# Sink scores as column tiles inside the score task, a re-planned opening, and a four-slot load ring in a fused attention and MLP kernel

## The chip, the cores and the metric

The kernel runs on one core of one Trainium2 chip. The metric is the device time of one execution in microseconds (us). A ratio between two kernels is the mean time of one kernel's fast runs over the mean of the other's in the same rounds, so it is not quite the ratio of the medians quoted beside it; its 95% interval stands in brackets. "Faster" and "slower" need 2%, which is 4.8 us here.

A word on noise: the kernel before, run again with every batch, spread from 240.66 to 242.19 us, and its median of a batch from 241.2 to 241.56.

## The reference

Four batches of eight heads, 768 positions of 64 dimensions. Each query sees a causal window of 128 keys and the first four keys of its sequence, the sinks. The attention's output goes through a layer norm and an MLP (512 to 2048, relu, back to 512), and is added to the MLP's result.

```python
scores = scale * np.matmul(q, k.transpose(0, 1, 3, 2))
is_sink = pos[None, :] < int(n_sink)                  # n_sink = 4
in_window = (rel >= 0) & (rel < int(window))          # window = 128
scores = np.where(is_sink | in_window, scores, -1e9)
a = softmax(scores); x = np.matmul(a, v)              # [B, S, H*D]
# ... then
xn = (x - mu) / np.sqrt(var + 1e-06) * g_ln
out = x + np.maximum(xn @ w_ch1, 0.0) @ w_ch2
```

## The kernel before

The work is cut into 24 blocks of 128 positions (six per batch), in six groups of four. A block loads query, key and value (float32 to bfloat16, one queue that GpSimd feeds), transposes query and key on TensorE into a bank of PSUM (the memory that this kernel's matmuls write to), copies them out, forms the scores of its own and the previous block's keys, takes exponentials on ScalarE, multiplies with the values, normalises on VectorE, subtracts the mean, and transposes the result for the MLP. The MLP of a group is 32 quanta of four 512-column matmuls each. The attention of the next groups is interleaved with those quanta. Blocks 0 to 3 have no MLP to hide behind; I call their stretch the opening.

What makes this kernel special is that the order is not written by hand. A small planner runs while the program is built. It knows an estimated cost of each task, a lag between engines, the slots of each ring of buffers and an estimated landing time of each load, and it always takes the task that can start first:

```python
for e, c in t["engines"].items():
    start = max([at, free[e]] + [done[d][1] if done[d][0] == e else done[d][2] for d in t["deps"]])
    k = (round(start, 3), t["prio"], start + c, i, e)
    if best is None or k < best:
        best = k
# ...
if t["land"] is not None:                     # a load
    dma_free = max(dma_free, start + 1.5) + t["land"]
    end = dma_free + 0.5
```

The result is a fixed list of instructions for each engine. Each engine runs its list in that order.

The parts that the change touches, cut:

```python
RINGS = dict(pa=4, ps=2, ld=10, qk=5, ks=2, vs=2, e=8, es=3, ...)   # pa: PSUM banks, ld: loads, qk: transposed tiles

def pk_(e, s, s2):                            # sink scores: a task of their own, full array
    for hp in range(4):
        nc.tensor.matmul(P["pk", t], lhsT=ks_of[b][:, hp], rhs=qkT[t][:, 0, hp, :],
                         start=(hp == 0), stop=(hp == 3))
# ... loads: blocks 0 to 3, W1 in four quarters, W2 in four quarters, then
for t in range(4, NT):
    load_block(t)
# ... pacing: the transposes of block t wait for an MLP quantum
for t in range(4, NT):
    n = 8 * (t - 4) - 8
    if n >= 0:
        plan.tasks[d_t[t]]["deps"].append(quanta[n])
```

The softmax here doesn't subtract the row's maximum and nothing guards it: scores larger than these inputs give would overflow.

## Time and profile before

| | before |
|---|---|
| time, median of 3 runs | 241.26 us (241.13 to 241.31) |
| span of the profiled run | 239.8 us |
| TensorE busy, and its share of the chain that ended last | 96%, 93% |
| first MLP matmul starts | 27.09 us |
| last matmul starts | 235.24 us |

TensorE is the bound as a whole, but a busy TensorE can be full of dummy matmuls (line L166, written to fill planned gaps), as in the opening. After 27.09 us nearly all of TensorE's time is work. The two ends of that stretch, the start of the first MLP matmul and of the last matmul, are the two numbers to follow: the opening is what lies before the first, and the stretch between them is 235.24 - 27.09 = 208.15 us. The tail after the last one is a VectorE operation and a store.

### The profile page before, as it was taken

Reading aid. Unit: us, or ns where it says so; the run is one execution under the profiler, and the core shown is the slowest. Engines: PE = TensorE matmul, PEld = TensorE weight load, DVE = VectorE, ACT = ScalarE, POOL = GpSimd, SP = SyncE. Lnnn points to the kernel's source line nnn. Section 1 sums busy time; section 2 is a strip of 40 time slices with the busy share of each in tenths; the row PEclk is TensorE's granted clock in tenths of the full one; section 3 lists DMA queues with packets and bytes.
Section 4 is the critical chain, followed back from the end, with each engine's and each line's share of the span. In section 5 each row is a group of like instructions: output and inputs, shape, how many; then the busy total and the mean of one; then the engine's idle time right before and its main releaser. Section 6 shows DMA issues by size and latency. Waiting matters only on the chain.

```text
span 239.8 us, 4795 instructions
## 1 busy us (share of the span) xinstructions
PE 231.4 (96%) x1957; PEld 129.4 (54%) x1989; DVE 137.5 (57%) x393; ACT 118.8 (50%) x179; POOL 76.3 (32%) x93
## 2 busy tenths in 40 slices
PE   8899999999999999999999999999999999999993
PEld 5676644666555555555556555456555555444441
DVE  7485801599997848746647568656667547200121
ACT  2167366655486632186751385643385760166000
POOL 8994237998989542340000000001000000100000
PEclk9999999999999999999999999999999999999998
DMA  7999999999999975991002110002110001200112
GB/s 46 138 162 205 206 204 158 151 178 183 182 179 153 126 52 107 109 105 7 3 8 80 46 44 4 0 2 88 44 48 0 3 0 67 77 34 0 44 44 87
DMA packets 82583, 20.23 MB, mean 84 GB/s; under 512 B 75393, under 2 KB 79489, under 8 KB 82562
## 3 DMA queue, kind: packets, MB, share of 16 engines
q0 software_dynamic: 79104, 13.64, 72.9%
q1 hardware_dynamic: 3458, 6.30, 7.1%
q8 instruction: 15, 0.25, 0.4%
q14 instruction: 6, 0.05, 0.1%
HBM read 27.27 MB, written 6.29 MB: 140 GB/s over the span
## 4 chain that ended last, share of the span: by engine, by line
PE 93%; DVE 4%; issue 1%; POOL 1%; POOLq 0%
PE ph L568 35%; PE pc L594 35%; PE ps L379 5%; PE pt L323 5%; PE px L531 3%; PE po L472 2%; PE po L475 2%; PE pk L447 2%; PE po L468 2%; PE ps L370 1%; DVE xc L500 1%; PE pt L166 1%; PE pv L427 0%; POOL qkn L255 0%; DVE xt L488 0%
## 5 line engine op out<-in xcount | busy, mean ns | idle before, releaser
L568 PE MATMUL ph<-xnt,w1s 128*128 128x512 bf16 x369 | 88.1, 379 | 0.9 <-issue 0.2
L594 PE MATMUL pc<-w2s,h 128*128 128x512 bf16 x367 | 87.1, 379 | 1.0 <-issue 0.2
L581 ACT ACTIVATE h<-ph 128x512 bf16<-128x512 f32 x85 | 50.8, 597 | 51.9 <-PE ph L568 51.9
L568 PEld LDWEIGHTS <-w1s 128*128 128x128 bf16 x384 | 35.5, 98 | 38.8
L594 PEld LDWEIGHTS <-h 128*128 128x128 bf16 x384 | 35.4, 98 | 37.0
L397 ACT ACTIVATE e<-ps 128x1024 bf16<-128x1024 f32 (+1 forms) x48 | 43.8, 955 | 18.2 <-PE ps L379 17.8
L606 DVE SCALAR_TENSOR_TENSOR ot<-pc,rsg,xt 128x512 f32<-128x512 f32 x24 | 18.0, 748 | 44.3 <-PE pc L594 35.3
L520 POOL TENSOR_TENSOR rsg<-ve,eps_half 128x4 f32<-128x4 f32 x6 | 6.5, 1086 | 96.2 <-DVE ve L518 96.2
L255 POOL DMA_DIRECT2D qkn<-in_q_dram x24 | 22.0, 916 | 22.8 <-PE pt L323 16.0
L329 ACT COPY qkT<-pt 128x1024 bf16<-128x1024 bf16 (+1 forms) x19 | 15.9, 862 | 16.9 <-PE pt L323 16.8
L260 POOL DMA_DIRECT2D qkn<-in_k_dram x24 | 21.9, 914 | 5.2 <-DMA w2s<-in_moe_w_ch_dram 3.4
L263 POOL DMA_DIRECT2D vn<-in_v_dram x24 | 22.0, 919 | 3.5 <-DMA w1s<-in_moe_w_ch_dram 1.7
L488 DVE SCALAR_TENSOR_TENSOR xt<-po,rc 128x256 bf16<-128x256 f32 x48 | 20.4, 424 | 1.7
L500 DVE SCALAR_TENSOR_TENSOR xc<-xt,sums,gb 128x512 bf16<-128x512 bf16 x24 | 18.0, 751 | 0.8
L406 DVE TENSOR_TENSOR e<-e,mask_std 128x1024 bf16<-128x1024 bf16 x28 | 18.1, 682 | 0.0
L485 DVE RECIPROCAL rc<-po 128x4 f32<-128x4 f32 x48 | 8.6, 179 | 14.6 <-PE po L475 12.5
L323 PE MATMUL pt<-ident,qkn 128*128 128x128 bf16 x192 | 16.0, 226 | 0.9 <-DVE qkT L329 0.9
L472 PE MATMUL po<-vn,e 128*128 128x65 bf16 x192 | 16.9, 194 | 0.0
L472 PEld LDWEIGHTS <-e 128*128 128x128 bf16 x192 | 14.4, 99 | 3.8
L509 DVE BATCH_NORM_STATS2 st<-xt 128x6 f32<-128x512 bf16 x24 | 16.3, 680 | 0.0
L579 DVE TENSOR_SCALAR h<-ph 128x512 bf16<-128x512 f32 x11 | 7.6, 688 | 15.1 <-PE ph L568 15.0
L329 DVE COPY qkT<-pt 128x512 bf16<-128x512 bf16 (+1 forms) x13 | 6.4, 502 | 16.6 <-PE pt L323 16.6
(75 smaller groups left out, 190.4 us busy)
## 6 DMA issues: line engine op xcount, KB each, us to landing
out_dram<-ot SPq DMA_DIRECT2D x24, 256.0 KB, 2.0
qkn<-in_q_dram POOLq DMA_DIRECT2D x24, 128.0 KB, 6.1
qkn<-in_k_dram POOLq DMA_DIRECT2D x24, 128.0 KB, 6.2
vn<-in_v_dram POOLq DMA_DIRECT2D x24, 128.0 KB, 6.1
w1s<-in_moe_w_ch_dram POOLq DMA_DIRECT2D x4, 512.0 KB, 10.6
w2s<-in_moe_w_ch_dram POOLq DMA_DIRECT2D x4, 512.0 KB, 17.8
g_row<-in_moe_g_ln_dram SPq DMA_DIRECT2D x1, 2.0 KB
```

Source lines behind the costliest of these rows:

```text
L255: nc.gpsimd.dma_start(qn[t][:, 0], q[b, :, rows, :].rearrange("h p d -> p h d"))
L260: nc.gpsimd.dma_start(qn[t][:, 1], k[b, :, rows, :].rearrange("h p d -> p h d"))
L263: nc.gpsimd.dma_start(vn[:, t, :, 0:64], v[b, :, rows, :].rearrange("h p d -> p h d"))
L323: nc.tensor.transpose(P["pt", t][:, aa, hp, :], qn[t][:, aa, 2 * hp:2 * hp + 2, :], ident)
L329: (nc.scalar.copy if e == "ACT" else nc.vector.tensor_copy)(qkT[t][:, sl], P["pt", t][:, sl])
L397: nc.scalar.activation(E[t, half][:, :, :, 0:nkb, :], P["ps", t, half][:, :, :, 0:nkb, :], AF.Exp, scale=scale)
L472: nc.tensor.matmul(po[:, hh, :], lhsT=ee[:, h % 2, hh // 2, 0, :], rhs=vn[:, t, h, :], start=(r < 2 and hh == 0), stop=(r == 0), skip_grou ...
L488: nc.vector.scalar_tensor_tensor(xt[t][:, 256 * half:256 * half + 256].rearrange("p (h d) -> p h d", h=4), in0=po[:, :, 0:64], scalar=1.0, ...
L500: nc.vector.scalar_tensor_tensor(xc[t], in0=xt[t], scalar=sums[t][:, 2:3], in1=gb, op0=ALU.subtract, op1=ALU.mult)
L568: nc.tensor.matmul(ph, lhsT=w1s[:, j, 128 * ht:128 * (ht + 1)], rhs=xnt[g][:, j, 0:n], start=(j == 0), stop=(j == NDM - 1))
L581: nc.scalar.activation(o, i, AF.Relu)
L594: nc.tensor.matmul(P["pc", t], lhsT=h1[g, ht][:, 128 * ti:128 * (ti + 1)], rhs=w2s[:, ht, :], start=(ht == 0), stop=(ht == NH1 - 1))
```

## The change

The intent: take TensorE cycles out of the sink scores by giving the four-key products only a 32-column slice of the array each, so that four run side by side; keep them in the score task; shorten the opening; and free the transposes from the pacing, so that fewer load buffers are needed. I call the way in which the array is divided its mode: the full array, row tiles (the scores, which use 64 rows each), or column tiles (the new sink scores). The diff, cut to its core:

```diff
-    RINGS = dict(pa=4, ps=2, ld=10, qk=5, ...)
+    LDN, QKN = 4, 5
+    RINGS = dict(pa=4, ps=2, ld=LDN, qk=QKN, ...)
 ...  # planner: rings counted one by one, a limit on queued descriptors, landing constants
-                for n_, (ring, key, readers) in enumerate(t["take"]):
+                for ring, key, readers in t["take"]:
+                    n_ = seen[ring] = seen.get(ring, -1) + 1
-                end = dma_free + 0.5
+                end = dma_free + (0.6 if t["lag"] is None else t["lag"])
 ...  # opening: the gain's broadcast and most masks after the first query; more warm-up dummies
+        g_ = plan.add({"PE": 1.0}, [d_q[0]], g1, (0, 0, 3), take=[("pa", "gb", 1)])
+        D["mb"] = plan.add({"DVE": .45}, [d_q[0]], make_masks_b, (0, 0, 1))
+        D["mc"] = plan.add({"DVE": 1.3}, [d_q[0]], make_masks_c, (0, 1, 5))
 ...  # query and key of the split blocks get a PSUM bank each
-            tk = plan.add({"PE": .23}, [d_k[t], tq], tr(1), (0, t, 1), drop=[("ld", t)])
-            ck = plan.add({"DVE": .43, "ACT": .59}, [tk, cq], cp(1), (0, t, 0), drop=[("pt", t)])
+            tk = plan.add({"PE": .23}, [d_k[t], tq], tr(1), (0, t, 1), take=[("pa", ("pt", t, 1), 1)], drop=[("ld", t)])
+            ck = plan.add({"DVE": .43, "ACT": .59}, [tk], cp(1), (0, t, 0), drop=[("pt", t, 1)])
 ...  # sink scores: behind the scores, in the same task, eight column tiles
+                if len(slots) > len(halves):
+                    for h2 in range(2):
+                        for hp in range(4):
+                            nc.tensor.matmul(P["pk", t][32 * hp:32 * hp + 32, h2, :], lhsT=ks_of[b][:, h2, hp, :],
+                                             rhs=qkT[t][:, 0, hp, :], start=(h2 == 0), stop=True,
+                                             skip_group_check=True)
 ...  # sink values: two half-width matmuls in place of one
-                    nc.tensor.matmul(po, lhsT=ES[t], rhs=vs_t[b][:, 4 * half:4 * half + 4, :],
-                                     start=True, stop=False, skip_group_check=True)
+                    for h2 in range(2):
+                        nc.tensor.matmul(po.rearrange("p (j a) c -> p j a c", a=2)[:, :, h2, :], lhsT=ES[t][:, h2, :],
+                                         rhs=vs_t[b].rearrange("p (j a) c -> p j a c", a=2)[:, 2 * half:2 * half + 2, h2, :],
+                                         start=(h2 == 0), stop=False, skip_group_check=True)
 ...
-    WARM0 = 24
+    WARM0 = 34
+    SINK = .16
 ...  # pacing: the scores, not the transposes
-            plan.tasks[d_t[t]]["deps"].append(quanta[n])
+            plan.tasks[d_s[t]]["deps"].append(quanta[n])
```

## The prediction

> **What bounds the kernel now.** I read the page first (busy shares, the chain's shares), then the table of stretches, then TensorE's order of time in the opening and in one steady stretch, then the end of the chain.
>
> ```profile
> span 239.8 us, 4795 instructions
> ...
> PE 231.4 (96%) x1957; PEld 129.4 (54%) x1989; DVE 137.5 (57%) x393; ACT 118.8 (50%) x179; POOL 76.3 (32%) x93
> ...
> PE 93%; DVE 4%; issue 1%; POOL 1%; POOLq 0%
> ```
>
> TensorE is busy for 96% and is 93% of the chain; no other engine passes 57%. The stretches (length, busy time of each engine, granted clock, DMA) show where the rest is:
>
> ```profile
> 5.60:12.60 7.00, 6.09 (x53) 4.59 (x53) 3.66 (x19) 1.19 (x2) 7.00 (x9) 1.00 2.14 136
> 12.60:27.10 14.50, 14.07 (x224) 10.05 (x223) 10.26 (x37) 9.19 (x13) 8.39 (x11) 1.00 1.43 190
> 27.10:38.00 10.90, 10.85 (x50) 4.94 (x52) 3.07 (x9) 6.92 (x12) 3.50 (x4) 1.00 1.44 197
> 38.00:100.00 62.00, 61.37 (x592) 35.85 (x602) 47.10 (x133) 34.26 (x53) 47.21 (x53) 1.00 1.92 147
> 100.00:208.00 108.00, 106.91 (x896) 58.72 (x911) 65.81 (x172) 56.37 (x83) 5.73 (x6) 1.00 0.14 34
> ```
>
> From 27.1 on TensorE is full. I checked this against its own work: 16 MLP matmuls of 512 columns take 68.97 to 72.44 in the steady lines below, 217 ns each, so 768 take 166.5 us; blocks 4 to 23 add about 40 us (per full block: transposes 0.45, sink scores 0.22, scores 0.55, value matmuls 0.71, transposes of the normalised rows 0.22). Sum 206.3 us against 235.64 - 27.5 = 208.1 us. Under 2 us of idling is left there, so a change of order can't gain more than that after 27 us; only fewer TensorE cycles can. The opening is different:
>
> ```profile
> 7.50 0.58 PE L323 MATMUL pt<-ident,qkn 128*128 128x128 bf16 x4 [0.91 <-DVE qkT L329]
> 7.88 1.06 PE L166 MATMUL pt<-ident 128*128 128x128 bf16 x8
> ...
> 17.07 0.67 PE L166 MATMUL pk<-ident 128*128 128x128 bf16 x9
> ...
> 24.14 1.61 PE L166 MATMUL px<-ident 128*128 128x128 bf16 x26
> 26.08 0.40 PE L531 MATMUL px<-ident,xc 128*128 128x128 bf16 x4 [0.33 <-DVE xc L500]
> 26.32 0.78 PE L166 MATMUL ph<-ident 128*128 128x128 bf16 x11
> 27.09 3.18 PE L568 MATMUL ph<-xnt,w1s 128*128 128x512 bf16 x13
> ```
>
> L166 is dummy work that fills planned gaps: 36+15+9+11+9+3 = 83 of them in the groups by form, at least 83 x 56 ns = 4.6 us. So the busy digit of the opening is not work, and the first MLP matmul comes at 27.09. The end is fixed: last matmul ends at 235.64, then 0.75 us of VectorE and a store, 4.1 us, untouched by the change.
>
> **What the Trainium skill says.** "TensorE: Matmul & The Clock Gate", section on packing small matmuls: outputs on different 32-partition strips of PSUM run at the same time in the array; it gives 2.38x for three column tiles. Nothing in this trace has column tiles, but the row-tiled scores do overlap: 16 of them in 0.55 us is 34 ns each with the switches, half of the 56 ns a 128-column matmul costs. "TensorEngine Tiling (Array Packing)", Key Properties: changing the tiling mode drains TensorE; Restrictions: column tiling switches the fast weight load off. The trace agrees on the drain:
>
> ```profile
> 67.88 0.39 PE L531 MATMUL px<-ident,xc 128*128 128x128 bf16 x4
> 68.10 0.39 PE L447 MATMUL pk<-qkT,ks 128*128 128x128 bf16 x4
> 68.42 0.62 PE L379 MATMUL ps<-qkT 64*128 64x128 bf16 x16
> 68.97 3.63 PE L568 MATMUL ph<-xnt,w1s 128*128 128x512 bf16 x16
> ```
>
> Start to start, four transposes take 0.22, but four sink scores ahead of row-tiled scores take 0.32, so 0.10 is the switch in; eight pairs of scores would take 0.45 and take 0.55, so another 0.10 is the switch out. The clock gate of the same TensorE page (half rate until some 3.4 us of sustained work) also shows, though the clock column reads 1.00 throughout: 8 dummies at 7.88 have a spacing of (1.06 - 0.29)/7 = 110 ns, 9 at 17.07 one of (0.67 - 0.22)/8 = 56 ns. The opening is planned with warm costs but runs cold for its first third.
>
> **The change, part by part.**
>
> Sink scores. Removed per block with sinks (16 of 24): four 128-column matmuls in the full array, 4 x 56 = 224 ns, in a task of their own. Added: eight matmuls of 32 output columns behind the scores, which at four at a time are two rounds of 56 = 112 ns, plus one more switch of mode, estimated from the 0.10 above. That is 0.21 against 0.22: nothing, if the switch costs in full. If row tiles to column tiles drain less (TensorE has to leave the row-tiled mode anyway), up to 0.11 is gained. I take 0.05 per block: 16 x 0.05 = 0.8 us, 0.7 of it in the steady part. The two half-width sink-value matmuls in place of one of 260 columns stream the same columns: about 0. The exponential grows from 128 to 256 columns: 0.28 us now, and 0.60 for 512, so 0.39: 16 x 0.11 = 1.8 us more on ScalarE, which is 50% busy; off the path outside the opening.
>
> Opening. Query 0 lands at 4.77 and key 0 at 6.33 (issue and landing of each load), but key 0 is transposed only at 7.50: VectorE runs the masks to 6.52 and the gain broadcast to 7.11, then copies query 0, and the key's transposes wait for that copy because both lie in one bank (the 0.91 in the line above). The change defers masks (twelve small operations to after the first load, eight mask_k ones gone), moves the broadcast (2.0 us of cold fp32 matmul, 3.66 to 5.67) behind query 0's transposes, and gives query and key a bank each. First scores should come some 1.3 us sooner: exponentials at about 8.8 instead of 10.15. More dummies (34 for 24) cover TensorE from 0.99 to about 4.6 without a hole and may warm it earlier.
>
> Then the planner: it modelled a task with two rings as needing a second free slot in the second ring, it modelled no queue limit, and half of the opening follows its order. In the trace block 2's query and key land at 10.66 and 11.49, yet its exponentials run at 18.76 to 20.87; block 3's land at 13.21 and 14.04, exponentials 21.35 to 23.59. The floor is ScalarE's chain. Block 1's exponentials (13.52 now) could start 2.3 us earlier, 11.2, since key 1 lands at 8.93. Six half-block exponentials follow; the last four of them now run from 18.76 to 23.59, 1.2 us apart, so 6 x 1.2 plus some 0.4 for the wider sink exponentials ends at 18.8. From the last exponential to the first MLP matmul the present trace takes 27.09 - 23.59 = 3.5 us (values, normalise, subtract, transpose, copy): 22.3. I add 0.7 for orders planned with warm costs: 23.0. Gain 27.1 - 23.0 = 4.1 us. TensorE's real work of the four blocks, about 12 us warm, fits between 5 and 20; the first quarter of the first weights lands at 20.23 and later quarters every 2.5 us against 3.5 us of use each, so weights don't hold it.
>
> Pacing and the four-block load ring. Transposes are freed from the MLP quanta and only scores are paced, so keys and queries wait as transposed tiles (five slots) instead of as loads (ten). Loads then run about eight blocks ahead of the scores, some 60 us at 8 quanta of 0.87 per block. TensorE doesn't wait on loads after 27 us now and should not then: worth 0. Split transposes of blocks 4 to 7 take two of four PSUM banks; I set aside 0.5 us of loss for this and for new short waits.
>
> Sum: 4.1 + 0.8 - 0.5 = 4.4 us. 241.3 - 4.4 = 236.9; I round to 237.0.
>
> **Rivals.** (1) Column tiles don't overlap or pay in weight loads: eight at 56 ns plus two switches, 0.65 instead of 0.22, costs 16 x 0.4 = 6.9 us and gives about 243. For: fast weight load is off. Against: row tiles overlap here, and the planner's own cost for the part went from 0.24 to 0.16. (2) The opening stays bound by ScalarE and VectorE (9.19 and 10.26 of 14.5 us), now with longer sink exponentials and the masks in between: first MLP matmul at 25.5, total about 239.5. For: the chain of the opening holds VectorE pieces between the matmuls. Against: 83 dummies, and 6 to 7 us between landing and exponential in blocks 2 and 3. (3) A wait appears in the steady part: PSUM banks (scores with sinks take one bank more at once), or the pow on POOL behind a stalled load; a stall of 0.2 us per block is 4 us and cancels the gain, 241. Against: TensorE waits for nothing there now. (4) All goes right, switch hidden: first MLP matmul at 22, sink 1.8 us: 234.5.
>
> **Range and chances.** The opening's gain I hold to 2 to 5.5 us, the sinks' to -1 to +1.8, the steady waits to 0 to 1.5 lost: 234.6 to 239.8. Two per cent is 4.83 us, 236.4, just past my centre; so 0.42 faster, 0.55 same, 0.03 slower (rivals 1 and 3 together with a poor opening).
>
> **What would show it.** First MLP matmul at about 23 and dummies outside the first run well under 83; the key's transposes not waiting for the query's copy; block 2 and 3 exponentials 3 to 4 us sooner. Scores plus sinks of a steady block from the first score to the next matmul 0.70 to 0.77 us (0.87 from the first sink score now). The stretch from the first MLP matmul to the last 0.5 us shorter or equal. Wrong if the opening ends after 25.5, if sinks take over 0.3, or if TensorE's idle time after the opening exceeds 3 us. In the tail nothing changes.

## The result, and the profile after

The changed kernel took 241.42 us (median of 4 runs, 241.2 to 241.84), the kernel before 241.28 in the same rounds (241.13 to 241.44). The ratio is 1.0008 [0.999, 1.0025]: the same. The prediction was 237.0, and its range of 234.6 to 239.8 does not hold the result.

| start of | before | after | difference |
|---|---|---|---|
| first MLP matmul | 27.09 | 25.56 | -1.53 |
| last matmul | 235.24 | 235.16 | -0.08 |
| the stretch between the two | 208.15 | 209.60 | +1.45 |

The opening did gain, about a third of what was predicted, and the stretch behind it gave the whole gain back. The page of the kernel after, its busy shares and the engines' shares of the chain that ended last:

```profile
span 239.7 us, 5054 instructions
...
PE 232.8 (97%) x2118; PEld 128.6 (54%) x2118; DVE 142.5 (59%) x390; ACT 117.2 (49%) x176; POOL 76.0 (32%) x92
...
PE 76%; DMA 11%; DVE 6%; POOL 5%; issue 1%; POOLq 0%
```

The busy shares hardly moved; the chain did. Before, TensorE had 93% of it, now 76%, and a transfer has 11%. A chain is followed back from the end, so a DMA in it means that something later waited for a landing, and that what lay before that landing on TensorE no longer counts. The same chain in order of time, around the opening's end (start, length, what):

```profile
22.86 16.67 DMA qkn<-in_k_dram
39.53 0.05 issue
39.58 0.40 PE pt L348 x4
...
61.08 0.44 DVE xt L518 x2
...
61.57 0.61 PE pt L348 x8
```

Until 39.53 us the chain does not run through the opening at all. It runs through the queue of loads: the key of block 4 was queued at 22.86 behind the second weights and landed at 39.53. After that, from 47.48 to 61.53 us, the chain is VectorE's own work piece after piece (the rows left out). So two things stand between the opening and the end that were not in the chain of before.

TensorE in order of time where that first wait is (start, length, engine, line, operation, tiles, count, and the idle time ahead of it with its releaser). Before:

```profile
40.03 0.39 PE L323 MATMUL pt<-ident,qkn 128*128 128x128 bf16 x4
...
41.12 0.39 PE L323 MATMUL pt<-ident,qkn 128*128 128x128 bf16 x4
```

After:

```profile
38.71 0.40 PE L348 MATMUL pt<-ident,qkn 128*128 128x128 bf16 x4
39.58 0.40 PE L348 MATMUL pt<-ident,qkn 128*128 128x128 bf16 x4 [0.46 <-DMA qkn<-in_k_dram]
```

Block 4's query and key land at 38.88 and 39.71 before, at 38.67 and 39.53 after: the queue is the same. Before, TensorE came to the transposes at 40.03 and 41.12, after both had landed. After, it came 1.3 us sooner, was through with the query's at 38.95 and stood until the key was there, 0.63 us; with the 0.20 us lost ahead of the query's, 0.83 us in all. (The view's 0.46 is counted from a modelled end of the matmuls; starts are measured, so I count from starts: 39.58 - 38.71 less the 0.24 that these four transposes take.)

The stretches of both kernels behind the opening (stretch, length, busy time and count of TensorE, weight loads, VectorE, ScalarE, GpSimd, then clock, DMA share, GB/s). Before:

```profile
27.10:44.00 16.90, 16.74 (x104) 8.40 (x108) 4.18 (x12) 10.80 (x19) 9.21 (x11) 1.00 1.79 182
44.00:65.00 21.00, 20.79 (x239) 12.99 (x243) 19.42 (x58) 12.44 (x19) 19.88 (x24) 1.00 2.27 176
```

After:

```profile
27.10:44.00 16.90, 16.39 (x108) 7.77 (x107) 2.93 (x9) 11.13 (x20) 11.04 (x13) 1.00 1.80 181
44.00:65.00 21.00, 20.69 (x269) 13.37 (x268) 19.68 (x56) 14.17 (x20) 18.14 (x22) 1.00 2.26 176
```

VectorE is third in each row. It is almost idle from 27.1 to 44 us in both (4.18 and 2.93 of 16.9 us), because block 4 and its successors have not landed, and nearly full from 44 to 65 (19.42 and 19.68 of 21 us). The MLP of group 1 can't start before VectorE has normalised blocks 4 to 7. There the changed kernel loses 0.9 us in five short waits from 59.7 to 62.2 us (by the trace four of them end with VectorE, which frees PSUM banks and normalised rows late, and one with ScalarE's sink exponential), against 0.2 before.

Adding up starts over the whole stretch, TensorE's work with the switches of mode is 207.4 us before and 207.55 after, waits are 0.8 and 2.05 (0.83 for block 4, the 0.9 near 60, 0.21 at 48.2, and small ones). So +0.15 is work and +1.25 is waiting.

The opening after, TensorE in order of time:

```profile
6.63 1.12 PE L307 MATMUL pg<-g_row,ones 1*128 1x512 f32 x2
7.68 0.40 PE L348 MATMUL pt<-ident,qkn 128*128 128x128 bf16 x4
...
8.36 0.67 PE L184 MATMUL pt<-ident 128*128 128x128 bf16 x9
...
15.58 0.59 PE L398 MATMUL ps<-neg_std,ident 128*128 128x512 bf16 x2
...
24.56 0.40 PE L561 MATMUL px<-ident,xc 128*128 128x128 bf16 x4 [0.33 <-DVE xc L530]
...
25.56 4.69 PE L599 MATMUL ph<-xnt,w1s 128*128 128x512 bf16 x21
```

The key's transposes at 7.68 no longer wait for a copy (0.91 us before). But they come no sooner than before (7.50): the gain's broadcast, moved behind the query's transposes, now stands ahead of them from 6.63, though key 0 landed at 6.37. And the first scores of block 2 come at 15.58, though its query and key landed at 10.56 and 11.40.

One thing did change early. The nine dummies at 8.36 start (0.67 - 0.22) / 8 = 56 ns apart; in the kernel before the eight at 7.88, shown in the prediction, start some 107 ns apart. By its starts TensorE keeps the slow distance up to 5.8 us in this profile and up to 12.5 in that of before, so part of the 1.53 us may come from there and not from the new order. No run separates the two.

And one steady block with sinks after, from the scores to the next MLP matmul:

```profile
67.97 0.62 PE L407 MATMUL ps<-qkT 64*128 64x128 bf16 x16
68.52 0.29 PE L414 MATMUL pk<-qkT,ks 128*32 128x128 bf16 x8
68.75 1.04 PE L599 MATMUL ph<-xnt,w1s 128*128 128x512 bf16 x4
```

From 68.52 to 68.75 the eight column-tiled matmuls and the way back to the full array take 0.23 us, where before four full-array matmuls took 4 x 56 ns = 0.224.

### The profile page after: what moved, and what is told of

Same layout as the page of the kernel before. It is cut to its first block, busy times and chain, and to the rows that moved or that the text cites. A ratio compares the mean times of both kernels' runs of the same rounds, so it can differ in the third digit from the quotient of the medians.

```text
span 239.7 us, 5054 instructions
## 1 busy us (share of the span) xinstructions
PE 232.8 (97%) x2118; PEld 128.6 (54%) x2118; DVE 142.5 (59%) x390; ACT 117.2 (49%) x176; POOL 76.0 (32%) x92
## 4 chain that ended last, share of the span: by engine, by line
PE 76%; DMA 11%; DVE 6%; POOL 5%; issue 1%; POOLq 0%
PE pc L625 32%; PE ph L599 29%; DMA qkn<-in_k_dram 7%; DMA w1s<-in_moe_w_ch_dram 4%; PE ps L407 4%; PE pt L348 3%; PE po L502 2%; PE px L561 2%; POOL qkn L270 2%; PE po L505 2%; POOL vn L278 1%; POOL qkn L275 1%; PE po L497 1%; DVE e L445 1%; PE pk L414 1%; DVE xt L518 1%
## 5 line engine op out<-in xcount | busy, mean ns | idle before, releaser
L625 PE MATMUL pc<-w2s,h 128*128 128x512 bf16 x384 | 90.4, 379 | 0.1
L599 PE MATMUL ph<-xnt,w1s 128*128 128x512 bf16 x384 | 89.2, 379 | 0.1
L612 ACT ACTIVATE h<-ph 128x512 bf16<-128x512 f32 x80 | 47.8, 597 | 42.3 <-PE ph L599 42.3
L550 POOL TENSOR_TENSOR rsg<-ve,eps_half 128x4 f32<-128x4 f32 x6 | 6.1, 1023 | 79.1 <-DVE ve L548 79.1
L576 ACT COPY xnt<-px 128x512 bf16<-128x512 bf16 x12 | 7.0, 585 | 36.0 <-PE px L561 36.0
L445 DVE TENSOR_TENSOR e<-e,mask_std 128x1024 bf16<-128x1024 bf16 x28 | 18.7, 685 | 4.9 <-ACT e L436 4.9
L354 DVE COPY qkT<-pt 128x512 bf16<-128x512 bf16 (+1 forms) x14 | 7.4, 536 | 22.6 <-PE pt L348 22.5
L610 DVE TENSOR_SCALAR h<-ph 128x512 bf16<-128x512 f32 x16 | 11.0, 690 | 11.1 <-PE ph L599 11.0
L354 ACT COPY qkT<-pt 128x1024 bf16<-128x1024 bf16 (+1 forms) x18 | 14.6, 838 | 2.2 <-PE pt L348 2.2
L348 PE MATMUL pt<-ident,qkn 128*128 128x128 bf16 x192 | 14.9, 219 | 0.7 <-DMA qkn<-in_k_dram 0.5
```

Source lines behind the costliest of these rows:

```text
L348: nc.tensor.transpose(P["pt", t, a][:, aa, hp, :], qn[t][:, aa, 2 * hp:2 * hp + 2, :], ident)
L354: (nc.scalar.copy if e == "ACT" else nc.vector.tensor_copy)(qkT[t][:, sl], P["pt", t, a][:, sl])
L445: nc.vector.tensor_mul(ee[:, :, 0:w], ee[:, :, 0:w], m[:, 0:w].unsqueeze(1).to_broadcast([128, 4, w]))
L599: nc.tensor.matmul(ph, lhsT=w1s[:, j, 128 * ht:128 * (ht + 1)], rhs=xnt[g][:, j, 0:n], start=(j == 0), stop=(j == NDM - 1))
L612: nc.scalar.activation(o, i, AF.Relu)
L625: nc.tensor.matmul(P["pc", t], lhsT=h1[g, ht][:, 128 * ti:128 * (ti + 1)], rhs=w2s[:, ht, :], start=(ht == 0), stop=(ht == NH1 - 1))
```

## The experiments

All were timed in five rounds against the kernel before, on one chip per batch. Three kernels give a wrong result (they are named so); the others are correct. The quoted texts name theories by letters; below each text it is said in words what was tried and which side the numbers came down on. The two questions were: why does the stretch give back what the opening gained, and why did opening and sinks gain less than predicted. Results first; "first MLP" is the start of the first MLP matmul in the profiled run.

| run | median us (range) | ratio to before | first MLP |
|---|---|---|---|
| after | 241.42 (241.2 to 241.84) | 1.0008 [0.999, 1.0025] | 25.56 |
| s_old | 241.07 (241.04 to 242.35) | 1.0004 [0.9982, 1.0026] | 25.97 |
| w_late | 242.09 (241.85 to 242.71) | 1.0034 [1.0018, 1.005] | 26.94 |
| p_tr | 242.15 (241.42 to 244.87) | 1.0045 [1.0008, 1.0082] | 25.78 |
| d_land | 241.17 (241.04 to 241.34) | 0.9991 [0.9977, 1.0005] | 26.04 |
| x_early2 | 240.71 (240.43 to 240.93) | 0.9971 [0.9955, 0.9986] | 25.88 |
| x_early2l | 241.99 (241.35 to 243.61) | 1.0031 [1.0002, 1.006] | 25.89 |
| dve_more | 243.71 (242.95 to 244.2) | 1.009 [1.0071, 1.011] | 25.50 |
| l_ten | 241.04 (240.71 to 242.05) | 0.9994 [0.9973, 1.0014] | 25.62 |
| c2 | 241.41 (240.99 to 242.69) | 0.9995 [0.9972, 1.0017] | 25.39 |
| o_nomask (wrong result) | 241.44 (241.25 to 243.75) | 1.0013 [0.998, 1.0046] | 24.60 |
| c2_nomask (wrong result) | 240.71 (240.38 to 242.45) | 0.9978 [0.9949, 1.0006] | 24.66 |
| o_vec | 241.29 (241.0 to 242.33) | 0.9999 [0.9977, 1.0022] | 25.87 |
| f_e2_24 | 240.34 (239.83 to 241.37) | 0.9962 [0.9944, 0.9981] | 25.65 |
| f_e1_12 | 239.70 (239.49 to 240.1) | 0.9935 [0.9921, 0.9949] | 25.62 |
| f_mix2_24 | 239.98 (239.36 to 240.42) | 0.9942 [0.9926, 0.9958] | 25.95 |
| f_mix3_24 | 239.50 (239.26 to 240.79) | 0.9934 [0.9914, 0.9954] | 25.86 |
| e1_nomask (wrong result) | 240.56 (239.3 to 242.09) | 0.9979 [0.9945, 1.0013] | 24.07 |
| e1_sold | 239.62 (239.25 to 241.05) | 0.9948 [0.9924, 0.9973] | 25.50 |

None of these reaches the 2% of "faster" or "slower": each counts as the same as the kernel before, and where I call one lower or higher I mean that its interval leaves out 1. A caution for all runs that change the plan's numbers, its dependencies or the order of loads (p_tr, d_land, both x_early2, c2, c2_nomask, the four f_ runs and the two built on one of them): the planner then also puts other tasks in another order. By the traces s_old, w_late, dve_more, l_ten and o_vec keep the order of TensorE's tasks, and o_nomask only leaves out its masks.

### First batch: sinks, opening, pacing, the plan's landings

**s_old** takes the change whole but for the sink scores, which stay in the score task and go back to four full-array matmuls, with the old masks and the single sink-value matmul.

```diff
-                    for h2 in range(2):
-                        for hp in range(4):
-                            nc.tensor.matmul(P["pk", t][32 * hp:32 * hp + 32, h2, :], lhsT=ks_of[b][:, h2, hp, :], ...)
+                    for hp in range(4):
+                        nc.tensor.matmul(P["pk", t], lhsT=ks_of[b][:, hp], rhs=qkT[t][:, 0, hp, :],
+                                         start=(hp == 0), stop=(hp == 3))
```

> The changed kernel with the old sink scores (four full-array matmuls, 128-wide exponential, one 260-column sink-value matmul) put in the same place, behind the scores; all else and the planned order as changed. Theory A (column tiles are cheaper than full-array matmuls in this place by about 0.10 us a block, which only pays for having moved behind the scores): first score to the next matmul after the sinks 0.88 us instead of 0.78, the stretch after the first MLP matmul 1.0 to 1.4 us longer, total 242.2 to 242.9. Rival B (the column tiles themselves cost what the opening gained): total 240.0 to 240.9.

Its TensorE at a steady block:

```profile
69.39 0.40 PE L423 MATMUL pk<-qkT,ks 128*128 128x128 bf16 x4
69.62 1.03 PE L604 MATMUL ph<-xnt,w1s 128*128 128x512 bf16 x3
```

From the sink matmuls to the next it is 69.62 - 69.39 = 0.23 us, as in the kernel after (68.75 - 68.52); theory A's 0.88 for scores and sinks did not hold, and the median, 241.07, lies in neither side's range for the total. Over the 14 blocks with sinks behind the opening, from starts of single instructions, medians, with the mean distance of two matmuls of a kind taken off each switch (28 ns for scores, 14 for column tiles, 56 for the full array): in the kernel after 0.118 us go to the switch out of row tiles, 0.090 to the eight matmuls and 0.138 to the switch from column tiles to the full array, in all 0.346; in s_old 0.120, 0.224 and 0.010, in all 0.354. The column tiles do overlap: four start some 3 ns apart and the next four 57 ns later, so they take 0.13 us less. The extra switch of mode costs that much, but for 8 ns. The times have two heaps here, four runs at 241.04 to 241.07 and two at 242.3; the profiled run is of the second, and in it block 4's key landed at 40.58, 1.05 us later than in the kernel after. That was the first hint that the landing sets the time.

**w_late** adds 27 dummy matmuls before the first MLP matmul.

```diff
+                for _ in range(27 * (g == 0 and ht == 0)):
+                    nc.tensor.matmul(ph[:, 0:128], lhsT=ident, rhs=ident, start=True, stop=True, skip_group_check=True)
```

> The changed kernel with 27 dummy matmuls (1.5 us) ahead of the first MLP matmul, so that the opening's gain is taken away. Theory A (TensorE gives the opening's gain back at waits near 39 us, for key 4, and near 60 us, for VectorE and banks): those waits shrink by as much, total 241.2 to 241.9. Rival C (the opening's gain is kept in full and something spread over the later part costs 1.5 us): total 242.7 to 243.1.

The first MLP matmul came 1.38 us later and the median 0.67 us: about half was absorbed, and 242.09 lies between the ranges of theory A and rival C. The wait at 39 us was gone, since TensorE now came after the landing, and some 0.8 us of waits near 60 stayed, where theory A had them shrink too. If the opening alone set the time, all of it would have come through.

**p_tr** paces the transposes with the MLP quanta, as before.

```diff
-            plan.tasks[d_s[t]]["deps"].append(quanta[n])
+            plan.tasks[d_t[t]]["deps"].append(quanta[n])
```

> The changed kernel with the MLP quanta pacing the transposes again instead of the scores. Rival D (freed transposes and their banks, run ahead, make the waits near 60 us): these waits of 0.9 us go, total 240.2 to 240.7. Theory A (the waits come from group 1 being ready late, whichever task is paced): total 241.2 to 242.2.

Pacing is not what costs: with the old pacing the kernel is no faster (1.0045), and waits of 0.10, 0.12 and some 0.5 us remain at 55 to 60.

**d_land** changes only the plan: the first quarter of the first weights is entered as 2.4 us longer, so that all later landings are expected later.

```diff
-        d_w1[c] = load(f, 2.56, desc=512)
+        d_w1[c] = load(f, 2.56 + (2.4 if c == 0 else 0), desc=512)
```

> The changed kernel with the planner told that the first weight chunk takes 2.4 us longer, as measured, so that key 4's transposes are planned after its true landing. Theory A1 (the 0.83 us at 39 us is only a misplaced task): the wait goes and the total falls to 240.4 to 240.8. Theory A2 (group 1's attention is the limit, so TensorE would only wait elsewhere, near 60 us): total 241.1 to 241.6.

The planner of the kernel after expects block 4's key at 37.08 us (its plan can be printed from the program; this is no measurement) and it landed at 39.53; it places the transposes in between. With the later landings in the plan the wait at 39 us is gone, but waits of 0.16, 0.27, 0.26, 0.46 and 0.30 us stand between 50 and 61, and the median is 0.25 us lower, in the range of theory A2. One wait became several; block 4 still arrives late for VectorE.

### Second batch: arrival and VectorE

**x_early2** loads blocks 4 and 5 ahead of the second weights. **x_early2l** does so and also has the 2.4 us of d_land.

```diff
+    for t in range(4, 6):
+        load_block(t)
     for c in range(4):
         load_w2(c)
-    for t in range(4, NT):
+    for t in range(6, NT):
         load_block(t)
```

> The changed kernel with the loads of blocks 4 and 5 ahead of the second weights instead of behind them, so that they land near 28 to 33 us instead of 38.7 to 43, while the second weights land 5.2 us later. Theory E (group 1's attention is late because its loads land late and VectorE, idle from 27 to 38 us, then can't catch up): the waits of 0.83 and 0.9 us near 39 and 60 us both go, total 239.3 to 240.0. Rival F (they only move, or the second weights come too late): total 241 or more.

> The same, with the planner told of the 2.4 us by which the weights really land later. Theory E: total 239.3 to 240.3. If misplaced tasks matter as well as the landing, this is 0.3 to 0.6 below x_early2; if not, the two agree within 0.3.

Earlier loads help a little: 0.9971, but 240.71 misses the range of theory E as well as that of rival F. TensorE still loses 0.24 + 0.11 us at 28 to 32, 0.31 at 44.9 and 0.28 at 63. With both edits the kernel got worse instead of better: block 6, now the first behind the second weights, is waited for, 1.57 us for its query and 0.65 for its key, up to 48.40 and 49.29. The combination was expected to add up, and it did not. The order of loads is that of x_early2, where block 6's query landed at 44.86 rather than 48.36. What differs, by the traces, is GpSimd's list: in this plan a small operation of GpSimd that waits for VectorE (the power in the norm, L550) stands ahead of the load of block 5's key. GpSimd idles 10.43 us there and issues that load at 30.24 (20.52 in x_early2), and all loads behind it come later. An order of loads is only as good as what else stands in the list of the engine that issues them.

**dve_more** does the mean subtraction of blocks 4 to 7 twice, 3.0 us more on VectorE.

```diff
-            nc.vector.scalar_tensor_tensor(xc[t], in0=xt[t], scalar=sums[t][:, 2:3], in1=gb,
-                                           op0=ALU.subtract, op1=ALU.mult)
+            for _ in range(2 if 4 <= t < 8 else 1):
+                nc.vector.scalar_tensor_tensor(xc[t], in0=xt[t], scalar=sums[t][:, 2:3], in1=gb,
+                                               op0=ALU.subtract, op1=ALU.mult)
```

> The changed kernel with the subtract of the mean done twice in blocks 4 to 7, 4 x 0.75 = 3.0 us more VectorE work in the stretch of 44 to 64 us, in the same order. Theory E (VectorE's chain sets when group 1 is ready): total 2.0 to 3.0 us longer, 243.4 to 244.4. Rival (VectorE has slack there and only banks or order hold TensorE): 241.4 to 242.1.

The median rose by 2.3 us for 3.0 us of VectorE work, and TensorE's waits grew, one at 62 us to 1.0. So in this stretch VectorE is on the path: an engine that is 59% busy over the span.

**l_ten** gives the load ring its ten slots back.

```diff
-    LDN, QKN = 4, 5
+    LDN, QKN = 10, 5
```

> The changed kernel with ten load buffers instead of four; the planned order of TensorE stays the same. All theories: the same within 0.3 us, 241.2 to 241.7, since no load is late because of a buffer. Rival (the small ring holds loads back that TensorE waits for): 240.8 or less.

Nothing: 0.9994. The four-slot ring costs nothing. But the order on TensorE is that of the kernel after, and its landing was another, so with other runs of the same order of tasks it gives a series:

| profiled run | key 4 landed | waits for block 4 | time of this run |
|---|---|---|---|
| l_ten | 38.93 | 0.18 | 240.71 |
| o_vec (told below) | 39.34 | 0.35 | 241.31 |
| after | 39.53 | 0.83 | 241.47 |
| s_old | 40.58 | 1.47 | 242.29 |

The time follows the landing: 1.65 us between the ends of the series against 1.58 us in time. These four also differ in their edits (two others of the same order, w_late and dve_more, add work and are left out), so the series by itself is no proof; o_nomask in the next batch is a test.

### Third batch: is the opening still on the path?

**o_nomask** leaves out the 16 matmuls that add masks in the opening. The result is wrong; the opening is shorter.

```diff
-                    if t in MPE:
+                    if t in MPE and False:
 ...
-                                                 start=(hh == 0 and kb == 0 and t not in MPE), stop=True,
+                                                 start=(hh == 0 and kb == 0), stop=True,
```

> The changed kernel without the sixteen mask matmuls of blocks 0 to 3 (a wrong result on purpose), the same order otherwise: the opening gets shorter by some 1 to 2 us. Theory E (after the opening the time is set by block 4's loads and VectorE): first MLP matmul at 23.8 to 24.6, total only 0 to 0.4 us less than the changed kernel, 241.0 to 241.5. Rival C (the opening counts one for one): total 239.5 to 240.4.

```profile
24.60 13.11 PE L599 MATMUL ph<-xnt,w1s 128*128 128x512 bf16 x58
38.95 0.40 PE L348 MATMUL pt<-ident,qkn 128*128 128x128 bf16 x4 [1.24 <-DMA qkn<-in_q_dram]
39.78 0.40 PE L348 MATMUL pt<-ident,qkn 128*128 128x128 bf16 x4 [0.43 <-DMA qkn<-in_k_dram]
```

This is the run that decides this question. The first MLP matmul came at 24.60, 0.96 us sooner than in the kernel after, and the time is 241.44 against 241.42: nothing arrived. The lines show where it went: TensorE stands for query and key of block 4, counted from starts 1.41 + 0.60 = 2.01 us in place of 0.83. So theory E, that an arrival of loads absorbs what the opening gains, held, and theory C fell. It also means that the 4.1 us of the prediction could not have come through in this order of loads even had the opening been that short.

**c2** loads blocks 4 and 5 early and corrects the planner's numbers by what the trace of the kernel after shows. **c2_nomask** is c2 without the opening's masks (wrong, edit as above).

```diff
+        land += {2: 0.6, 3: 0.7, 13: W1X}.get(n_, 0.0)          # W1X = 0.8
-            x_ = plan.add({"PE": cost * len(halves) / 2 + .15 + SINK * sink},
+            x_ = plan.add({"PE": cost * len(halves) / 2 + .15 + SINK * sink + .06},
-            d_ks[b] = plan.add({"DVE": .3}, ...
+            d_ks[b] = plan.add({"DVE": .75}, ...
-    SINK = .16
+    SINK = .23
+    for t in range(4, 6):
+        load_block(t)
```

> The changed kernel with the loads of blocks 4 and 5 ahead of the second weights, and with the planner's numbers set to what the trace shows (landings of the first loads and weights, the switch of mode, the copies of sink keys). Theory E (late landing of group 1's loads and tasks planned against wrong landings cost the 0.83 and 0.9 us): both waits go, total 239.4 to 240.3, better than both kernels. Rival: the waits only move, as in x_early2l: 240.8 or more.

> c2 without the mask matmuls of blocks 0 to 3 (a wrong result on purpose). Theory E: with the loads of blocks 4 and 5 early, most of a shorter opening is kept: total 0.7 to 1.6 us below c2. If the total stays within 0.3 of c2, group 1 is limited by something else than its first loads.

c2 missed its expectation: 241.41, no better than the kernel after. In the profiled run, its slowest (242.69), TensorE stood 1.75 us up to 48.26 for block 6's key, which landed at 48.22. It lost some 1.4 us more just behind the opening: the granted clock reads 0.50 from 25.48 to 28.90, and MLP matmuls follow each other at six distances of 427 ns and one of 327 instead of 216. TensorE had idled 1.78 us ahead of 24.47 and 0.52 ahead of 25.39, where the kernel after runs dummies (77 of them in this plan, 106 there). That a plan with better means has less slack and breaks at the next late landing is my reading; it was not tested. c2_nomask was 0.7 us below c2 with a first MLP matmul 0.73 us sooner (25.39 and 24.66), so here the opening came through; but the spread of both is larger than that, c2_nomask has the same two idle gaps of 1.78 and 0.52 us and no fall of the clock, and it still waited 0.83 + 0.66 us for block 6. I take no more from this pair than that the wait for block 4 was gone.

**o_vec** puts the copies of blocks 2 and 3 on VectorE, to test whether ScalarE's copies delay the opening's exponentials.

```diff
-                (nc.scalar.copy if e == "ACT" else nc.vector.tensor_copy)(qkT[t][:, sl], P["pt", t, a][:, sl])
+                (nc.scalar.copy if e == "ACT" and t not in (2, 3) else nc.vector.tensor_copy)(qkT[t][:, sl], P["pt", t, a][:, sl])
```

> The changed kernel with the query and key copies of blocks 2 and 3 done by VectorE where the plan had ScalarE; TensorE's order unchanged. Theory G (ScalarE's four copies hold back block 2's exponentials in the opening): these start at 15.4 to 15.9 instead of 16.55 and the first MLP matmul comes at 24.5 to 25.1. Rival (TensorE's planned order holds the scores): first MLP matmul within 0.3 us of 25.56, or later. Total in either case within 0.5 us of the changed kernel.

ScalarE where block 2's first exponential starts, in the kernel after:

```profile
16.55 1.02 ACT L436 ACTIVATE e<-ps 128x1024 bf16<-128x1024 f32 x1
```

and in o_vec:

```profile
16.85 1.02 ACT L436 ACTIVATE e<-ps 128x1024 bf16<-128x1024 f32 x1 [3.03 <-PE ps L407]
```

The theory's numbers fell. ScalarE is free of copies and stands idle for 3.03 us ahead of this exponential, which starts 0.30 us later than with them. It waits for TensorE's scores. The edit isn't clean, since the four copies now burden VectorE; but in the kernel after, too, the scores end at 16.51, by their modelled end, and the exponential follows at 16.55, so ScalarE's copies held it up by a few hundredths at most. In TensorE's fixed order block 2's scores stand behind the transposes and values of block 1, and these wait for VectorE (0.45 us ahead of 13.94 in the kernel after).

### Fourth batch: order of loads and a margin together

By now the reading was: block 4 must arrive sooner, without putting others too late, and the plan must not place work right at an expected landing. What was still open was whether the two together give the opening's gain back, or whether VectorE's full stretch keeps it anyway. Each kernel takes an order of loads and adds a margin to the planned landing; the code counts loads, and the margin starts with the 21st load of the queue, so the first four loads behind the first weights, block 4's among them, have none.

```diff
-                end = dma_free + (0.6 if t["lag"] is None else t["lag"])
+                end = dma_free + (0.6 if t["lag"] is None else t["lag"]) + t.get("slack", 0.0)
 ...
+        n_loads[0] += 1
+        plan.tasks[i]["slack"] = SLACK if n_loads[0] > 20 else 0.0
 ...
-    for c in range(4):
-        load_w2(c)
-    for t in range(4, NT):
-        load_block(t)
+    for w_, n_ in (("b", 4), ("w", 0), ("w", 1), ("w", 2), ("w", 3), *(("b", t) for t in range(NT))):
+        if w_ == "w" or n_ not in d_v:
+            (load_w2 if w_ == "w" else load_block)(n_)
```

This is **f_e1_12**: block 4 ahead of the second weights, `SLACK = 1.2`. **f_e2_24** has blocks 4 and 5 ahead of them, **f_mix2_24** the order 4, two quarters of weights, 5, two quarters, and **f_mix3_24** 4, 5, two quarters, 6, two quarters; these three have `SLACK = 2.4`.

> As x_early2 (loads of blocks 4 and 5 ahead of the second weights), with the planner taking every load from block 4 on as usable 2.4 us later. Theory H (misplaced tasks): the wait near 45 us goes, total 239.6 to 240.3. Theory I (the queue is too late in any order): 240.6 or more, with the wait elsewhere.

> Block 4's loads alone ahead of the second weights, and a margin of 1.2 us. Theory H: 239.8 to 240.6. Theory I: 240.6 or more.

> Order block 4, two chunks of the second weights, block 5, the other two chunks; margin 2.4 us. Theory H: 239.6 to 240.3. Theory I: 240.6 or more.

> Order blocks 4 and 5, two chunks of the second weights, block 6, the other two chunks; margin 2.4 us. Theory H: 239.4 to 240.2, the lowest of the four. Theory I: 240.6 or more, with a wait for the last weight chunks.

All four lie below the kernel before, by 0.4 to 0.7%, and their intervals lie below 1. No median reaches theory I's 240.6, so theory I fell; theory H held in direction (two medians lie in its ranges, f_e1_12 is 0.1 us better, f_e2_24 is 0.04 above). What the margin adds to the order is not shown: f_e2_24 and x_early2, the same order of loads with and without it, have ratios of 0.9962 and 0.9971 with overlapping intervals, and block 4 alone ahead was not run without a margin. f_e1_12 is the steadiest, 239.49 to 240.1. Its stretches and TensorE's first transposes of block 4:

```profile
27.10:44.00 16.90, 16.80 (x129) 8.79 (x130) 8.62 (x23) 10.73 (x18) 10.91 (x13) 1.00 1.71 186
44.00:65.00 21.00, 20.74 (x258) 13.33 (x261) 17.96 (x53) 14.14 (x19) 18.61 (x22) 1.00 2.29 178
```

```profile
25.62 2.75 PE L603 MATMUL ph<-xnt,w1s 128*128 128x512 bf16 x11
28.20 0.39 PE L352 MATMUL pt<-ident,qkn 128*128 128x128 bf16 x4
```

The opening ends at 25.62, as in the kernel after. But block 4 is transposed at 28.20 rather than 38.71, VectorE has 8.62 us of work in the stretch where it had 2.93, and has 17.96 rather than 19.68 in the full one. No wait above 40 ns is left behind the opening, and TensorE has 91% of the chain that ended last (76% in the kernel after). The stretch from the first MLP matmul to the last is 207.55 us, which is the 207.55 of work that I had counted in the kernel after, without the 2.05 of waits. The other three keep a wait: 0.34 us at 60 in f_e2_24, 0.59 for block 4's query at 29 in f_mix2_24, 1.06 for the same in the profiled run of f_mix3_24, which was its slowest (240.79).

### Fifth batch: the two other terms on top of the better kernel

**e1_nomask** is f_e1_12 without the opening's mask matmuls (wrong), **e1_sold** is f_e1_12 with the old sink scores. The edits are those of o_nomask and s_old.

> f_e1_12 without the sixteen mask matmuls of blocks 0 to 3 (a wrong result on purpose). Theory: with the waits gone the opening counts; first MLP matmul near 24.6, total 0.6 to 1.1 us below f_e1_12, 238.6 to 239.1. If group 1 still sets the time: within 0.3 us of f_e1_12.

> f_e1_12 with the old sink scores (four full-array matmuls, 128-wide exponential, one sink-value matmul) in the same place. Theory: the extra switch of mode costs what the column tiles save, so within 0.4 us of f_e1_12, 239.3 to 240.1. If column tiles do pay: 240.5 or more; if they cost: 239.0 or less.

e1_nomask missed its expectation. The first MLP matmul came at 24.07, 1.55 us sooner than in f_e1_12, and the median is 0.86 us higher. In the profiled run, one of its two longest (242.0), TensorE stood 2.37 us up to 29.02 for block 4's query, which landed at 28.98 and had no margin in the plan:

```profile
29.02 0.45 PE L352 MATMUL pt<-ident,qkn 128*128 128x128 bf16 x4 [2.21 <-DMA qkn<-in_q_dram]
29.26 1.91 PE L603 MATMUL ph<-xnt,w1s 128*128 128x512 bf16 x4
```

It is the o_nomask finding once more, one load earlier: shortening the opening moves TensorE to the next arrival. And the wait cost more than its length. The four MLP matmuls behind it take 1.91 us where four take 1.03 elsewhere: the granted clock reads 0.50 from 29.23 to 32.65, as in c2, and MLP matmuls start 427 ns apart. The stretch is 4.05 us longer than in f_e1_12, 2.37 by the wait and the other 1.7 by the half clock. So this run is no clean test of the opening's worth; what sets off the fall of the clock is left open (o_nomask stood 1.41 us without one). Its fastest run, 239.3, is no better than the fastest of f_e1_12, 239.49, by more than 0.2 us.

e1_sold came out as expected for neutral sinks: 239.62 against 239.70 (ratios 0.9948 and 0.9935, whose intervals overlap), its stretch is 207.44 against 207.55 us, and switches and sink scores take 0.354 against 0.346 us per block, as in s_old and the kernel after. So on a kernel without waits, where a TensorE cycle counts in full, the column tiles are worth nothing.

## Why the prediction was wrong

**The opening's floor (the step "Six half-block exponentials follow ... 1.2 us apart").** It gave a first MLP matmul at 23.0; it came at 25.56. Block 1's exponentials did start early, at 11.64 (11.2 was predicted), and from the last exponential's end at 22.24 to the first MLP matmul it took 3.3 us (3.5 predicted). What failed lies between: block 2's first exponential started at 16.55 and not close behind block 1's. I took the spacing from the last four exponentials of the trace before and stretched it over all six, as if ScalarE alone set it. In TensorE's fixed order block 2's scores stand behind work of block 1 that waits for VectorE; o_vec, with ScalarE free, started them no sooner. The first link failed too: block 0's exponentials were to start at 8.8, 1.3 us sooner, and started at 9.76 (10.15 before), because the moved broadcast took the place of the wait ahead of key 0's transposes. This is rival (2) in its opening, which had 25.5, though not in its total of 239.5. Which single wait inside the opening is the longest link I did not settle; TensorE's own work is part of it, since without the sixteen mask matmuls it ended 0.96 us (o_nomask) and 1.55 us (e1_nomask) sooner. The dummies, which I had as evidence of slack, were 106 and not "well under 83": they show gaps that the planner foresees, not time that another order can have.

**The steady stretch (the step "TensorE doesn't wait on loads after 27 us now and should not then: worth 0", with 0.5 set aside).** It lost 1.25 us in waits. The step took the absence of waits before as a reserve. It was not one: query 4 landed at 38.88 and TensorE came for it at 40.03, key 4 at 39.71 and 41.12, reserves of 1.15 and 1.4 us, while I predicted an opening 4.1 us shorter. The landings were all in the profile. I compared the weights' landings with their use, but not block 4's. Had I done so, I would have seen that no more than about 1.2 us of any opening gain could pass 41 us unchanged. The o_nomask run shows such a ceiling: another 0.96 us off the opening gave nothing.

The second layer of it is VectorE: 57% busy over the span and so set aside, but 19.42 of 21 us busy just behind the late blocks, which was to be seen in a table of shorter stretches than the 62 us one I printed. dve_more shows that work there comes through at 2.3 us for 3.0. Rival (3), a wait in the steady part that cancels the gain, is in the end what happened; I had put it on PSUM banks and a stalled pow and argued "TensorE waits for nothing there now". The releasers are block 4's landing first, then VectorE and the banks that it frees.

**The sinks (0.8 us, from "I take 0.05 per block").** The sum beside it was right: two rounds of 56 ns and one more switch, 0.21 us against 0.22. From the first sink matmul to the next matmul it is 0.228 us, and 0.234 with the old sinks in the same place (s_old). The hope that leaving row tiles for column tiles costs less, the only ground for the 0.05, did not hold: it took 0.118 us, as leaving for the full array did (0.120). The two half-width sink-value matmuls, which I had at 0, cost a little: 3.32 against 3.13 us over the 28 pairs. Together work rose by 0.15 us where 0.7 of fall was predicted.

**What held.** The key's transposes don't wait for the query's copy (though they came no sooner); the added dummies did bring TensorE to its 56 ns earlier, or it came with them; the sink exponential takes 0.38 us (0.39 predicted); the ring of four slots costs nothing (l_ten); the tail is unchanged. The condition named as proof of error, "if the opening ends after 25.5", was met, by 0.06 us. Two readings in the working are off without bearing on the result: the stretch in its check of TensorE's work starts at 27.09 and not at 27.5, and the slow spacing of the opening lasts to 12.5 us of 27, nearer half than a third. The half rate shows there, but not the 3.4 us that the prediction cites beside it: TensorE was busy with hardly a gap from 1.0 to 6.4 us, and the slow spacing went on for 6 us more. In the kernel after it ended after 4.8 us.

In terms of the sum: 4.1 + 0.8 - 0.5 = 4.4 was predicted, and 1.53 - 0.15 - 1.25, about 0.1, came of it in the two profiled runs. The opening's term was the largest miss and the waits made it final: f_e1_12, with this opening and these sinks but no waits, is 1.7 us below the kernel before in its batch (241.39 - 239.70).

What stays open: what holds the opening at 25.56 link by link, and how much of its gain is due to the earlier full spacing; whether the order of loads alone, without a margin and without the new order of other tasks that comes with it, gives f_e1_12's gain; why landings of the same queue differ by up to a microsecond and more from run to run (38.93 to 40.58 for the same load), and how much of the medians' scatter comes from that alone.

## What to carry to other kernels

A gain in one stage is worth only as much as the distance to the next fixed arrival behind it; so before counting it, set the landing of each load that comes next beside the moment its reader asks for it, and look at the busiest engine in the short stretch that follows. Where a plan fixes the order of each engine, loads that have time to spare (here the second weights) belong behind those that have none, and a work item placed right at an expected landing will wait in some runs, since landings scatter (by 1.65 us here); a margin of 1.2 us stood in the best of these kernels, though what it alone gave was not measured. Look also at what stands in the list of the engine that issues the loads. Before tiling small matmuls, count the switches of mode: saving 0.13 us of matmuls for one switch of 0.14 is no gain.

## What the Trainium skill lacked or had wrong

- "TensorEngine Tiling (Array Packing)", Tiling Modes, Key Properties says that a change of tiling mode drains TensorE and gives no time. Here, beyond the spacing of the matmuls themselves, full array to row tiles took 0.096 us, row tiles to column tiles 0.118, row tiles to full array 0.120, and column tiles to full array 0.138.
- "TensorE: Matmul & The Clock Gate", Part 3 on packing gives 2.38x for three column tiles of 512 columns and about 4 ns of issue per tile. The overlap agrees (some 3 ns between the starts of four tiles), but for eight matmuls of 128 columns the switch takes nearly all of it: 0.346 us per block with them and 0.354 without.
- No page says what spread of landings to plan for when a queue of loads is kept full: the same load landed between 38.93 and 40.58 us in runs of the same order, and two loads in a row landed 0.83 to 0.86 us apart.
